# A one-core FNet and low-rank mixer kernel: warm-up products, evacuation, W2's queue and the residual table rearranged in the front

## The chip, the cores and the metric

The kernel runs on one core of one Trainium2 chip. The metric is the device time in microseconds of that core, as the median of several runs. A profiled execution gives the times of single instructions, measured from its own first instruction.

## What is computed

The input x has shape (8, 3136, 256). An FNet layer takes the real part of the two-dimensional Fourier transform over sequence and channels; a mixer follows, with a low-rank product over the sequence (U of 3136 x 32, V of 32 x 3136) and a two-layer MLP over the channels (256 to 1024 to 256), each with its residual:

```
X = np.fft.fft(np.fft.fft(x, axis=1), axis=2).real
h = X.transpose(0, 2, 1) @ U @ V
u = X + h.transpose(0, 2, 1)
out = u + np.maximum(u @ w_ch1, 0) @ w_ch2
```

## The kernel before

The sequence length 3136 is split as 49 x 64 (N1, N2). The transform is done as products with tables of sines. Those tables are made on the chip: VectorE or GpSimd computes an angle as an integer phase, a bit mask takes it modulo a full turn (mask_bits, L427), and ScalarE's sine gives the table (sin_of, L431). The eight batches are handled as four pairs. The first batch of pair 0 goes through a front of its own, because nothing else can cover it; from pair 0's second batch on, the stages are placed between the MLP products of the batches before (plan, L731).

The order of the instructions is written out by hand: manual_schedule (L456) leaves each engine's instructions in the order of the program. So an instruction that waits holds everything that comes after it on its engine or queue. SP and GpSimd issue most loads; GpSimd also computes.

The front (L458 to L675) runs in this order:

- X0, the first batch, is loaded in pieces by load_single (L104), most of them from GpSimd's queue. U is loaded into uf, cast into ub by ScalarE (L525 to L527). Then TensorE gets 28 products of 128 columns into a scratch tile (L533), whose values nobody uses.
- VectorE computes the angles of the tables ua (L536 to L553), Fs and F32 (L557 to L577), ScalarE takes the sines (L555, L569, L578). TensorE multiplies ua with ub (upss) and transposes ua (tpss), 25 products each (L585 to L590). line32 (L198) forms line 32 of the batch with F32; its output lies in a free corner of tpss. Nine unused products follow in tps0 (L594). ScalarE copies upss to us, VectorE copies tpss to T (L595 to L597) and mirrors it (L598).
- quarter_products (L214) are 64 products on X0 for each of four rounds r, into the tiles tps. Each tile is evacuated into one of the staging tiles zts (L609), two rounds to each; then quarter_rows (L236) copies them with a shift of rows into g0, eight copies for each staging tile (L612, L613). Round r's evacuation alternates between VectorE and ScalarE.
- The staging tiles zts and the raw W1 tiles w1_f share memory (the tags w1_f0 and w1_f1), so that each half of W1 (L621) can be loaded only when its staging tile has been read. GpSimd's order here is: a one-element copy that waits for the first evacuation (gate, L615), two loads of V (L616, L617), the two halves of W1. W2 is loaded from SP's queue (L622).
- Six unused products of 512 columns (L646) precede te_single (L293), which multiplies g0 with us; te_out (L267) copies the result into te, and spread (L302) repeats te into the lower half of g0. v_rows (L625) fills T's lower half from V: rows 0 to 8 on ScalarE, the rest on GpSimd.
- lines (L324) are the sequence products of the first eight columns, in four groups: once with g0's upper half (L654), then with te (L657); after each group, move (L334) copies it to q. w1_fold (L636) multiplies W1 with a channel transform table Q, and ScalarE scales it into W1p (L642). w2_fold (L515) adds and subtracts the two halves of W2 on VectorE.
- residual_tables (L442) computes on GpSimd the phases qa of the table Bp and its signs sg; bp_mask and bp_sin are its mask on VectorE and its sine on ScalarE. Then X1, the pair's second batch, is loaded from GpSimd's queue (L669 to L673).

The main loop takes chunks of up to 512 columns of q: mlp1 (L372) makes four pairs of product tiles hps with W1p, each of which ScalarE turns into hT by a ReLU (L382); mlp2 (L384) multiplies hT of the chunk before with W2 and q with Bp, and stores the result. Scratch tiles in PSUM of the front come from a pool of four buffers (bank2, L474), handed out in turn; a tile waits until the readers of the tile four before it are done.

Of the kernel before, what the change touches and what calls it, by code (L numbers as in the profile page):

```python
# [22 lines left out]
def kernel(  # L23
# [9 lines left out]
    nc = tc.nc  # L33
# [3 lines left out]
    P = 128  # L37
# [17 lines left out]
    F32 = cpool.tile([PR, 3, 32], FP16)  # L55
# [16 lines left out]
    def copy_act(o, i):  # L72
        nc.scalar.copy(o, i)  # L73

    def copy_dve(o, i):
        nc.vector.tensor_copy(o, i)  # L76
# [121 lines left out]
    def line32(b, ps=None, start=True):  # L198
        ps = ps if ps is not None else psd.tile([P, 2, D], FP32, tag="ps", name="ps32")
        o, y = ps[0:32, 0], x32[b]  # L200
        for i, (oc, t, yc) in enumerate([(o[:, 0:129], 0, y[:, 0:129]), (o[:, 1:128], 0, y[:, 255:128:-1]),
                                         (o[:, 129:256], 1, y[:, 1:128]), (o[:, 129:256], 2, y[:, 255:128:-1])]):
            nc.tensor.matmul(oc, F32[:, t], yc, start=(start and i == 0), stop=True, skip_group_check=True)

        def out():
            z32 = cpool.tile([32, D], BF16, name=f"z32_{b}")
            nc.scalar.copy(z32[:], o)
            return z32
        return out

    def row32(g, z32):
        nc.sync.dma_start(out=g[63:64, 0:NK1, :], in_=z32[0:NK1])

    def quarter_products(X, ps, i0, n):  # L214

        for i in range(n):
            for m in range(2):
                for q in range(4):
                    d = 32 * q + i0 + i
                    o = ps[32 * q:32 * q + 32, i]  # L220
                    w = X[0:PR, :, (256 - d if d else 128) if m else d]
                    if d:
                        f, oc = Fs[:, 0:3:2 if m else 1, :, 0:NK1] if m else Fs[:, 0:2, :, 0:NK1], o[:, :, :, 0:NK1]
                    else:
                        f, oc = Fs[:, 0, :, 0:NK1], o[:, m, :, 0:NK1]
                    nc.tensor.matmul(oc, w, f, start=(i % 4 == 0 and m == 0), stop=True, skip_group_check=True)
# [9 lines left out]
    def quarter_rows(g, zt, i0, engines):  # L236

        n = zt.shape[4]
        for q in range(4):
            d0 = 32 * q + i0  # L240
            for c in range(2):
                r = 32 - c
                engines[2 * q + c](g[32 * c:32 * c + r].rearrange("p k (s d) -> p k s d", s=2)[:, :, :, d0:d0 + n],
                                   zt[32 * q:32 * q + r, c])
# [179 lines left out]
    def tmp(shape, name, dt=FP32):  # L424
        return pool.tile(shape, dt, name=name, tag=name)

    def mask_bits(a, bits):  # L427

        nc.vector.tensor_scalar(a.bitcast(I32), a.bitcast(I32), (1 << bits) - 1, None, op0=AL.bitwise_and)

    def sin_of(o, a, bits):  # L431

        nc.scalar.activation(o, a.bitcast(I32), AF.Sin, scale=-2.0 * math.pi / (1 << bits) * (1.0 - 2.0 ** -21),
                             bias=pi[0:a.shape[0]])
# [7 lines left out]
    def residual_tables(eng):  # L442
        pq = cpool.tile([P, 4], FP32, name="pq")
        qa = ypool.tile([P, 2, P], FP32, tag="y", name="qa")
        for blk in range(2):
            o = pq[:, blk:blk + 1]
            eng.tensor_scalar(sg[:, blk:blk + 1], pf[:], 64.5 - blk, None, op0=AL.is_ge)
            eng.tensor_scalar(o, sg[:, blk:blk + 1], -64.0, pf[:], op0=AL.mult, op1=AL.add)
            eng.tensor_scalar(o, o, 2.0 / D, blk / D, op0=AL.mult, op1=AL.add)
            eng.tensor_scalar(pq[:, 2 + blk:3 + blk], sg[:, blk:blk + 1], 0.25, 128.25, op0=AL.mult, op1=AL.add)  # L450
            eng.tensor_scalar(qa[:, blk], jf[:, 0:P], o, pq[:, 2 + blk:3 + blk], op0=AL.mult, op1=AL.add)
        eng.tensor_scalar(sg[:], sg[:], -2.0, 1.0, op0=AL.mult, op1=AL.add)
        return lambda: mask_bits(qa[:], 16), lambda: sin_of(Bp[:], qa[:], 16)
# [20 lines left out]
    def bank2(shape, name):  # L474
        return fpool.tile([P, *shape], FP32, tag="f", name=name)
# [4 lines left out]
    idle = W1m[0][:].rearrange("p a j -> p (a j)")[:, 0:640]  # L480
    nc.vector.memset(idle.bitcast(FP32), 0.0)

    wps = bank2([1024], "warm")
# [31 lines left out]
    def w2_fold(i):  # L515
        nc.vector.tensor_tensor(W2[:, :, i * P:(i + 1) * P], w2_f[:, :, 0], w2_f[:, :, 1],
                                op=(AL.subtract if i else AL.add))

    zts = [pool.tile([P, 2048], BF16, name=f"zt{i}", tag=f"w1_f{i}")[:, 0:64 * NK1].rearrange(
        "p (c k s i) -> p c k s i", c=2, k=NK1, s=2) for i in range(2)]  # L520
    g1 = gpool.tile([P, NK1, D], BF16, tag="g1", name="w2_f")
    w2_f = g1[:, 0:16].bitcast(FP32).rearrange("p (t s) d -> p t s d", s=2)

    ub = tmp([P, NK1, 2, R], "ub", BF16)
# [4 lines left out]
    idn = tmp([64, 64], "idn", FP16)  # L529
    ts(idn[:], jf[0:64, 0:64], pf[0:64], None, AL.is_equal)  # L530

    for i in range(28):
        nc.tensor.matmul(wps[:, 0:P], ub[:].rearrange("p k s r -> p (k s r)")[:, 0:P], idle[:, P:2 * P], start=True, stop=True)  # L533

    pk = tmp([P, 4], "pk")
    ts(pk[:, 0:1], pf[:], -1.0, 127.0)  # L536
# [35 lines left out]
    an2 = tmp([PR, 3, 32], "an2")  # L572
# [2 lines left out]
    for i in range(3):  # L575
        ts(an2[:, i], jf[0:PR, 0:32], pv[:, 6:7], pv[:, 7 + i:8 + i])
    mask_bits(an2[:], 16)  # L577
    sin_of(F32[:], an2[:], 16)  # L578
    mask_bits(jq[:], 16)
    Q = tmp([P, 3, P], "Q", FP32R)  # L580

# [2 lines left out]
    tpss = [bank2([16, 64], "ttps") for i in range(2)]  # L584
    for k in range(NK1):  # L585
        nc.tensor.matmul(upss[k // 16][0:64, k % 16], ua[:, k], ub[:, k], start=(k % 8 == 0), stop=True,
                         skip_group_check=True)
    for k in range(NK1):
        nc.tensor.matmul(tpss[k // 16][0:64, k % 16], ua[0:64, k], idn[:], start=(k % 8 == 0), stop=True,
                         skip_group_check=True)  # L590
    z32 = line32(0, tpss[1][:, 12:16].rearrange("p k (a d) -> p a (k d)", a=1), False)
    tps0 = bank2([8, 2, 2, 32], "tps")
    for i in range(9):
        nc.tensor.matmul(tps0[:, 0].rearrange("p s c k -> p (s c k)"), idle[:, 0:P], idle[:, P:2 * P], start=True, stop=True)  # L594
    for i, (k0, k1) in enumerate([(0, 16), (16, NK1)]):  # L595
        copy_act(usv[:, k0:k1], upss[i][0:64, 0:k1 - k0])
        copy_dve(T[0:64, k0:k1, 0:64], tpss[i][0:64, 0:k1 - k0])  # L597
    nc.vector.tensor_copy(T[0:64, :, 64:128], T[0:64, :, 63::-1])  # L598
    z32 = z32()
    sin_of(Q[:, 0:2], jq[:], 16)  # L600
    nc.scalar.mul(Q[:, 2], Q[:, 1], -1.0)

    g0 = gpool.tile([P, NK1, D], BF16, tag="g0", name="g")
    first.g[0] = g0
    row32(g0, z32)
    for r, evac in enumerate([copy_dve, copy_act, copy_dve, copy_act]):
        ps = bank2([8, 2, 2, 32], "tps") if r else tps0
        quarter_products(X0, ps, 8 * r, 8)
        evac(zts[r // 2][:, :, :, :, 8 * (r % 2):8 * (r % 2) + 8].rearrange("p c k s i -> p s c k i"),  # L609
             ps[:, :, :, :, 0:NK1].rearrange("p i s c k -> p s c k i"))  # L610
        if r == 2:
            quarter_rows(g0, zts[0], 0, [copy_dve] * 8)  # L612
    quarter_rows(g0, zts[1], 16, [copy_dve] * 6 + [copy_act] * 2)  # L613
    gate = tmp([1, 2], "gate")
    nc.gpsimd.tensor_copy(gate[:, 0:1], zts[0][0:1, 0, 0, 0, 0:1])  # L615
    nc.gpsimd.dma_start(out=uv[64:96], in_=moe_V)  # L616
    nc.gpsimd.dma_start(out=uv[96:128], in_=moe_V)  # L617
# [1 line left out]
    for c in range(2):  # L619
        w1_f.append(pool.tile([P, 2, 512], FP32R, name=f"w1_f{c}", tag=f"w1_f{c}"))  # L620
        nc.gpsimd.dma_start(out=w1_f[c][:], in_=moe_w_ch1.rearrange("(h p) j -> p h j", p=P)[:, :, c * 512:(c + 1) * 512])  # L621
    nc.sync.dma_start(out=w2_f, in_=moe_w_ch2.rearrange("(t p) (s d) -> p t s d", p=P, s=2))  # L622
    Vk = uv.rearrange("p (k2 k1) -> p k1 k2", k1=N1)

    def v_rows(lo, hi, act=False):  # L625
# [10 lines left out]
    def w1_fold(c, ps=None):  # L636
        ps = ps or bank2([2, 512], "w1ps")
        for blk in range(2):
            for f in range(2):
                nc.tensor.matmul(ps[:, blk], Q[:, 2 if f and blk else blk], w1_f[c][:, f],  # L640
                                 start=(f == 0), stop=(f == 1))
        nc.scalar.mul(W1p[c][:], ps[:], 0.5)  # L642

    teps = bank2([2, D], "teps")
    for i in range(6):
        nc.tensor.matmul(teps[:].rearrange("p a d -> p (a d)"), idle[:, 0:P], idle[:, P:640], start=True, stop=True)  # L646
    te_single(first, 0, lambda g, te: None, teps)
    s3b0 = list(s3_steps(first, 0, copy_alt))
# [1 line left out]
    groups = [(g, blk) for g in range(2) for blk in range(2)]  # L650
    pst = [bank2([2, 2, 256], "ps") for i in range(2)]
    pss = [pst[i // 2][:, i % 2] for i in range(4)]
# [2 lines left out]
    w1_fold(0)  # L655
    for ps, (g, blk) in zip(pss, groups):
        lines(ps, g, blk, P, tes[0])  # L657
        move(ps, g, blk, copy_dve if blk else copy_act)
    w1_fold(1)
    spread([(nc.vector, 8, 16)])(g0, tes[0])  # L660
# [2 lines left out]
    v_rows(17, NK1)  # L663
    w2_fold(0)
    w2_fold(1)
    bp_mask, bp_sin = residual_tables(nc.gpsimd)
    bp_mask()
    bp_sin()
    loads = load_single(1)  # L669
# [100 lines left out]
    for i in range(len(chunks) + 1):  # L770
        cur = chunks[i] if i < len(chunks) else None
        prv = chunks[i - 1] if i else None
        if cur is not None:
            p = cur.p
# [42 lines left out]
```

## Time and profile before

| | us |
|---|---|
| median of 14 runs | 476.11 |
| lowest, highest | 473.68, 478.27 |
| profiled execution, its own time | 476.77 |
| span of its instructions | 475.0 |
| TensorE (products) busy | 436.1 |
| ScalarE busy | 296.3 |
| VectorE busy | 223.9 |
| GpSimd busy | 144.0 |
| mean granted TensorE clock, as a share of full speed | 0.968 |

An instruction line of the timeline gives the start, the length, the engine, the line of the program, the operation, what it writes and reads, how many were merged, and in brackets how long the engine stood idle before it and who released it. PE is TensorE, PEld its weight loads, DVE VectorE, ACT ScalarE, POOL GpSimd, SP the engine that only issues loads and stores; a q behind the name means its queue. The chain of waits follows the work that ended last back to the start. DMA figures are the busy share of the core's 16 DMA engines and the GB/s that they moved.

### The profile page before, as it was taken

To read this page: it belongs to the slowest core of one execution; us is meant where nothing else is said; L and a number is where in the kernel's file an instruction comes from. 1 tells how busy PE (TensorE), PEld (TensorE's weight loads), DVE (VectorE), ACT (ScalarE), POOL (GpSimd) and SP (SyncE) were. 2 spreads that over 40 slices of the span, in tenths; PEclk is the share of its full clock that TensorE was granted. 3 is DMA by queue.
4 is the path that set the end of the run, shared out by engine and by line. 5 is a ranking of instruction groups with operands and counts; after the bars stand their busy time and mean duration, and the time that the engine had idled before them with its cause. 6 is when DMAs were issued, how large, how long until landed. Compare 5 with 4: busy or idle time off the path is not lost.

```text
span 475.0 us, 10551 instructions
## 1 busy us (share of the span) xinstructions
PE 436.1 (92%) x4167; PEld 315.7 (66%) x4229; DVE 223.9 (47%) x537; ACT 296.3 (62%) x422; POOL 144.0 (30%) x156
## 2 busy tenths in 40 slices
PE   3677899699998998999999999999999999999995
PEld 3654566476775776776777776776777777776773
DVE  7624346777633547545344346647254344311212
ACT  5533688566755565777646656677655656666662
POOL 6168434485133026346060035544050000000000
PEclk9855999999999999999999999999999999999998
DMA  8732775459549355777396365586493333333424
GB/s 148 174 99 43 117 201 148 112 168 248 162 121 228 73 144 145 216 209 221 98 167 162 85 177 157 152 249 188 113 179 69 71 68 68 68 66 73 90 51 89
DMA packets 59714, 64.35 MB, mean 135 GB/s; under 512 B 12902, under 2 KB 52624, under 8 KB 59504
## 3 DMA queue, kind: packets, MB, share of 16 engines
q1 hardware_dynamic: 49904, 42.28, 38.4%
q0 software_dynamic: 7280, 14.70, 13.3%
q10 hardware_dynamic: 2480, 6.69, 3.8%
q8 instruction: 33, 0.54, 0.5%
q14 instruction: 17, 0.14, 0.1%
HBM read 34.62 MB, written 32.19 MB: 141 GB/s over the span
## 4 chain that ended last, share of the span: by engine, by line
PE 72%; DVE 8%; DMA 6%; ACT 4%; issue 4%; POOL 3%; SPq 2%; DVEq 0%; POOLq 0%; ACTq 0%
PE hps L380 29%; PE ops L391 29%; PE ps L322 4%; PE ops L394 4%; DMA out_dram<-ob 4%; ACT hT L382 3%; PE ps L184 2%; SPq L406 2%; DVE g L76 1%; DMA g<-zturn 1%; PE teps L284 1%; DVE ob L402 1%; DVE q L76 1%; DVE yb L135 1%; DVE ob L401 1%
## 5 line engine op out<-in xcount | busy, mean ns | idle before, releaser
L382 ACT ACTIVATE hT<-hps 128x1024 bf16<-128x1024 f32 (+1 forms) x208 | 202.3, 975 | 122.1 <-PE hps L380 113.4
L391 PE MATMUL ops<-W,hT 128*128 128x256 bf16 x1568 | 224.9, 273 | 0.7 <-DVE ob L402 0.3
L391 PEld LDWEIGHTS <-hT 128*128 128x128 bf16 x1568 | 145.1, 98 | 35.4 <-DVE ob L402 0.8
L401 DVE TENSOR_TENSOR ob<-ops,om 128x256 f32<-128x256 f32 (+1 forms) x102 | 42.2, 413 | 193.3 <-ACT om L400 188.2
L380 PE MATMUL hps<-q,W1p 128*128 128x512 bf16 (+1 forms) x420 | 105.7, 362 | 5.3 <-DVE q L76 1.4
L380 PE MATMUL hps<-q,W1m 128*128 128x512 bf16 x351 | 95.4, 379 | 2.1 <-ACT hT L382 0.5
L143 POOL TENSOR_TENSOR y<-xa,xb 98x1020 f32<-98x1020 f32 (+1 forms) x24 | 55.3, 2305 | 124.8 <-DMA xa<-in_x_dram 90.2
L76 DVE CAST q<-ps 128x512 bf16<-128x512 f32 (+2 forms) x120 | 64.4, 558 | 37.7 <-PE ps L322 30.0
L380 PEld LDWEIGHTS <-W1p 128*128 128x128 bf16 x448 | 41.2, 99 | 31.8 <-issue 7.1
L380 PEld LDWEIGHTS <-W1m 128*128 128x128 bf16 x384 | 35.3, 98 | 26.5 <-issue 1.4
L394 PEld LDWEIGHTS <-q 128*128 128x128 bf16 x392 | 38.4, 98 | 20.8
L400 ACT COPY om<-ops 128x256 f32<-128x256 f32 (+1 forms) x102 | 37.1, 364 | 8.4 <-PE ops L391 8.1
L402 DVE TENSOR_TENSOR ob<-ops,om 128x256 f32<-128x256 f32 (+1 forms) x102 | 41.1, 403 | 0.0
L322 PE MATMUL ps<-T,g 128*128 128x128 bf16 (+3 forms) x400 | 38.6, 225 | 1.8 <-DMA g<-zturn 1.3
L306 POOL COPY g<-te 64x1024 int32<-64x1024 int32 (+1 forms) x22 | 22.8, 1082 | 51.7 <-DVE te L270 48.3
L394 PE MATMUL ops<-Bp,q 128*128 128x128 f16 x200 | 38.4, 219 | 0.0
L73 ACT CAST z<-ps 128x512 bf16<-128x512 f32 x48 | 28.2, 587 | 16.0 <-PE ps L184 15.7
L394 PE MATMUL ops<-Bm,q 128*128 128x128 f16 x192 | 36.9, 219 | 0.0
L322 PEld LDWEIGHTS <-g 128*128 128x128 bf16 (+1 forms) x400 | 30.7, 102 | 7.3 <-issue 2.9
L99 POOL DMA_INDIRECT xb<-in_x_dram,idx x24 | 25.5, 1064 | 5.4 <-issue 4.5
L134 DVE TENSOR_TENSOR yb<-y 98x508 bf16<-98x508 f32 (+1 forms) x24 | 24.7, 1030 | 0.9 <-POOL y L143 0.8
L184 PE MATMUL ps<-yb,F 98*128 98x258 bf16 (+1 forms) x108 | 18.9, 265 | 5.4 <-DVE q L76 4.3
(137 smaller groups left out, 224.3 us busy)
## 6 DMA issues: line engine op xcount, KB each, us to landing
out_dram<-ob SPq DMA_DIRECT2D x389, 64.0 KB
xa<-in_x_dram SPq DMA_DIRECT2D x24, 392.0 KB
g<-zturn SPq DMA_DIRECT2D x6, 800.0 KB
zturn<-z ACTq DMA_DIRECT2D x9, 512.0 KB
X<-in_x_dram POOLq DMA_DIRECT2D x4, 384.0 KB, 7.5
X<-in_x_dram POOLq DMA_DIRECT2D x2, 744.0 KB, 8.2
zturn<-z ACTq DMA_DIRECT2D x3, 448.0 KB
w_f<-in_moe_w_ch_dram SPq DMA_DIRECT2D x1, 1024.0 KB
```

What stands on the lines that cost most here:

```text
L73: nc.scalar.copy(o, i)
L76: nc.vector.tensor_copy(o, i)
L143: nc.gpsimd.tensor_tensor(ck.y[:, 0:n, 1:256], ck.xa[:, 0:n, 1:256], rb[:, :, 255:0:-1], op=AL.add)
L184: nc.tensor.matmul(o[..., cs], F[:, 2 * t + i].rearrange("p b k c -> p (b k c)"), y[..., cs], start=first, stop=True, skip_group_check=True)
L322: nc.tensor.matmul(o, lt, r, start=st, stop=True, skip_group_check=True)
L380: nc.tensor.matmul(ps[:, i, 0:n], (W1p if ch.sg > 0 else W1m)[jp // 2][:, blk, j], q[:, blk, c0:c0 + n], start=(blk == 0), stop=(blk == 1))
L382: nc.scalar.activation(ch.h[:, 2 * jp:2 * jp + 2, 0:n], ps[:, :, 0:n], AF.Relu)
L391: nc.tensor.matmul(ps, ch.h[:, j, t * P:(t + 1) * P], W2[:, j, :], start=(j == 0 and (t % 2 == 0 or last)), stop=(j == JT - 1), skip_group ...
L394: nc.tensor.matmul(ps[:, j], q[:, j, tk], (Bp if ch.sg > 0 else Bm)[:, j], start=False, stop=False, skip_group_check=True)
L400: nc.scalar.copy(om[:, 0:n], ch.po[:, 0:n, 1])
L401: nc.vector.tensor_tensor(ob[:, 0:n, 0:P], ch.po[:, 0:n, 0], om[:, 0:n], op=AL.add)
L402: nc.vector.tensor_tensor(ob[:, 0:n, P:D], ch.po[:, 0:n, 0], om[:, 0:n], op=AL.subtract)
```

## The change

The unused products before the tables become six of 512 and twenty of 64 columns. Nine unused products in tps0 give way to twelve in a free corner of the tile tpss[1], ahead of line32. The F32 sine and line32 move between the first and second pair of copies. Of the four evacuations, ScalarE takes three instead of two, and VectorE one; the row copies of the first staging tile follow after round 1 instead of round 2; of those of the second, ScalarE takes three instead of two. The residual table's GpSimd part moves ahead of the quarter products, behind a one-element copy that waits for the mask of an2; its mask and sine stay where they were. W2's load moves from SP's queue to GpSimd's, behind W1. The unused products before te_single become fourteen. The lines with te are issued in one loop, and their moves in another.

```diff
-    for i in range(28):
-        nc.tensor.matmul(wps[:, 0:P], ub[:].rearrange("p k s r -> p (k s r)")[:, 0:P], idle[:, P:2 * P], start=True, stop=True)
+    ubw = ub[:].rearrange("p k s r -> p (k s r)")[:, 0:P]
+    for w in [512] * 6 + [64] * 20:
+        nc.tensor.matmul(wps[:, 0:w], ubw, idle[:, P:P + w], start=True, stop=True)
...
-    sin_of(F32[:], an2[:], 16)
     mask_bits(jq[:], 16)
...
-    z32 = line32(0, tpss[1][:, 12:16].rearrange("p k (a d) -> p a (k d)", a=1), False)
+    for i in range(12):
+        nc.tensor.matmul(tpss[1][:, 9:11], idle[:, 0:P], idle[:, P:2 * P], start=True, stop=True, skip_group_check=True)
     tps0 = bank2([8, 2, 2, 32], "tps")
-    for i in range(9):
-        nc.tensor.matmul(tps0[:, 0].rearrange("p s c k -> p (s c k)"), idle[:, 0:P], idle[:, P:2 * P], start=True, stop=True)
     for i, (k0, k1) in enumerate([(0, 16), (16, NK1)]):
         copy_act(usv[:, k0:k1], upss[i][0:64, 0:k1 - k0])
         copy_dve(T[0:64, k0:k1, 0:64], tpss[i][0:64, 0:k1 - k0])
+        if i == 0:
+            sin_of(F32[:], an2[:], 16)
+            z32 = line32(0, tpss[1][:, 12:16].rearrange("p k (a d) -> p a (k d)", a=1), False)
...
+    gate = tmp([1, 2], "gate")
+    nc.gpsimd.tensor_copy(gate[:, 1:2], an2[0:1, 0, 0:1])
+    bp_mask, bp_sin = residual_tables(nc.gpsimd)
...
-    for r, evac in enumerate([copy_dve, copy_act, copy_dve, copy_act]):
+    for r, evac in enumerate([copy_dve, copy_act, copy_act, copy_act]):
...
-        if r == 2:
+        if r == 1:
             quarter_rows(g0, zts[0], 0, [copy_dve] * 8)
-    quarter_rows(g0, zts[1], 16, [copy_dve] * 6 + [copy_act] * 2)
-    gate = tmp([1, 2], "gate")
+    quarter_rows(g0, zts[1], 16, [copy_dve] * 5 + [copy_act] * 3)
...
-    nc.sync.dma_start(out=w2_f, in_=moe_w_ch2.rearrange("(t p) (s d) -> p t s d", p=P, s=2))
+    nc.gpsimd.dma_start(out=w2_f, in_=moe_w_ch2.rearrange("(t p) (s d) -> p t s d", p=P, s=2))
...
-    for i in range(6):
+    for i in range(14):
         nc.tensor.matmul(teps[:].rearrange("p a d -> p (a d)"), idle[:, 0:P], idle[:, P:640], start=True, stop=True)
...
         lines(ps, g, blk, P, tes[0])
+    for ps, (g, blk) in zip(pss, groups):
         move(ps, g, blk, copy_dve if blk else copy_act)
...
-    bp_mask, bp_sin = residual_tables(nc.gpsimd)
```

## The prediction

> **What bounds the kernel now.** I read the overview slices first, then the chain of waits, then the timeline of the front, then the clock by window.
>
> The overview has TensorE busy nine tenths or more in most slices of 11.9 us, but not in the first five and the eighth, and the granted clock at half speed in slices three and four (24 to 48 us):
>
> ```profile
> PE   3677899699998998999999999999999999999995
> ...
> PEclk9855999999999999999999999999999999999998
> ```
>
> So after 50 us the kernel is one long TensorE program, and a microsecond won in the front should reach the end. What ends the front? The chain of waits, in order of time (start, length, what), around the start of the main loop:
>
> ```profile
> 31.97 2.07 POOL T L498
> ...
> 35.26 2.07 POOL T L498
> ...
> 37.40 0.68 POOL sg L447
> ...
> 38.18 2.26 POOL pq L448
> ...
> 43.09 0.42 DVE qa L429
> ...
> 43.95 1.01 ACT hT L382
> ```
>
> GpSimd copies V's rows into T until 37.3, then builds the residual table (37.40 to 43.05), VectorE masks it, ScalarE takes the sine, and only then comes the first ReLU of the main loop. The timeline shows who was ready earlier:
>
> ```profile
> 38.02 2.36 DVE L516 TENSOR_TENSOR W<-w_f 128x1024 bf16<-128x1024 f32 x2
> ...
> 39.39 0.59 PE L380 MATMUL hps<-q,W1p 128*128 128x512 bf16 x1 [1.11 <-ACT W1p L642]
> ...
> 43.53 0.51 ACT L433 ACTIVATE Bp<-qa,pi 128x256 f16<-128x256 int32 x1 [4.20 <-DVE qa L429]
> ...
> 43.95 1.92 ACT L382 ACTIVATE hT<-hps 128x1024 bf16<-128x1024 f32 x2
> ```
>
> The products for that ReLU began at 39.39; ScalarE stood 4.20 us at the sine, which is ahead of the ReLU in its order. **The first ReLU, at 43.95, is the mark against which I cost everything.** The clock, in windows of 1 us (PE, PEld, DVE, ACT, POOL busy, clock, DMA):
>
> ```profile
> 14.00:15.00 1.00, 0.57 (x6) 0.57 (x6) 0.97 (x3) 1.00 (x3) 0.00 (x0) 0.71 0.04 5
> ...
> 17.00:18.00 1.00, 1.00 (x63) 1.00 (x57) 0.86 (x1) 0.00 (x0) 0.00 (x0) 0.58 0.41 122
> ...
> 24.00:25.00 1.00, 0.39 (x2) 0.00 (x0) 0.96 (x4) 0.00 (x0) 0.67 (x1) 0.83 0.42 96
> ...
> 48.00:49.00 1.00, 1.00 (x5) 0.43 (x4) 0.45 (x1) 0.40 (x1) 0.41 (x2) 0.72 1.10 222
> ```
>
> A clock that is 1 or 0.5 must have switched at 14.42 (down), 17.84 (up), 24.66 (down) and 48.56 (up) to give these means. The distances are 1, 2 and 7 times 3.41 us.
>
> [...] the table's first pq step took 2.26 us under the W2 fold, its twin at 41.81 took 0.27; and the W1 load issued at 24.33 moved little until VectorE's row copies ended at 25.99 (39 GB/s at 25 to 26 us, 225 in the next). [...]
>
> **The change, part by part.**
>
> *Early warm-up (L533).* 28 products (3.17 us, 7.16 to 10.33) become 6 of 512 and 20 of 64 columns. From 113 ns for 128 columns there, 6 x 4 x 0.107 + 20 x 0.055 = 3.7 us, to 10.9; the next operand (ua) is ready at 10.87. Cost 0 to 0.3 us, hidden by the sine.
>
> *Order on ScalarE at 12 us.* The us copy no longer stands behind the F32 sine (12.83). Fs ends at 11.93, so us (1.27 us) runs 12.0 to 13.2 instead of 13.2 to 14.39, and the bank of tps0 is free 1.2 us sooner. The nine products of L594 (1.12 us) leave the path; twelve others stand at 12.8 to 14.1 at the latest, in another bank, in front of line32. Quarter products start at about 14.0 instead of 15.48; X0 must have landed, and its traffic falls away at 13 to 14 us. Gain 1.5 us; with the half clock of 14.42 to 17.84 avoided, up to 0.8 more.
>
> *Evacuation and row shifts.* Before: VectorE did two evacuations (0.99 each) and 14 row copies (0.36), the last ending at 25.99. Now r0 is VectorE's, r1 to r3 ScalarE's (0.83). With 64 products in 1.13 to 1.4 us: r1 done at 16.3, evacuated at 17.1; eight row copies to 20.0; r3 evacuated at 19.4; then VectorE 5 x 0.36 to 21.9, ScalarE 3 x 0.86 to 22.0. g0 complete at 22.0 instead of 26.0: gain 4.0 us.
>
> *Fourteen 512-column products (L646).* 14 x 0.22 = 3.0 us at full clock from 18.6: to 21.6, hidden by the row copies. Without that cover: 6.0 us at half clock, and a stall like the 2.28 us that TensorE showed at 21.1 with no releaser. Then they end at 27.
>
> *te, lines, W1 folds.* At full clock te_single is about 1.7 us (50 took 1.59 to 1.7 at 89.92) against 2.89; lines 0.9 (four took 0.22 at 50.75) against 1.78; a fold, at twice the clock, 1.0 against 2.07. Splitting lines from moves removes TensorE's waits of 1.20 and 0.67 us on ScalarE's copies. Summed from 22.0: te 23.7, W1 fold 26 (W1's first half issued at 20.1 when zt0 is free, 4.7 us to land as before), lines 27, second fold 28; ScalarE after V's rows (26.7): first W1p 27.7, two moves to 28.9, second W1p to 29.9. Main products could begin at about 30 instead of 39.4, and a ReLU at 31.
>
> *Residual table early.* Its twelve GpSimd instructions cost 5.65 us where they stood; the uncontended half (41.49 to 43.05) says 3.3 in all. From 13.0, after the gate on an2 (12.79), they end at 16.5 to 17.2, in GpSimd's idle time (9.6 to 18.2). Queued behind them: V's loads, whose own gate opens at about 16.4. They go out at 17.2 instead of 18.33, land 7.1 us later at 24.3, and V's first rows (2.4 us on ScalarE) are done by 26.7. On the late side GpSimd goes from V's rows straight to X1's loads: X1 is issued at about 33 to 36 instead of 43.65; it landed at about 55 (last issue 47.8, 7.5 to land), 9 us ahead of its first use at 64.58, and that moves up with everything.
>
> *W2 behind W1.* The issue leaves SP (0.44 us; nothing stands behind it there until the stores at 54.38) and joins GpSimd's queue after W1's second half, which waits for zt1 (22.0). W1 goes out at 22.0 to 22.8, W2 to 23.6; the spread behind it waits for te (24.5) anyhow: 0 us. But the landing matters: the mask on VectorE stays behind the two W2 folds, and the sine and every ReLU behind the mask. No row shows W2 from this queue. Bounds: 1.05 MB of W1 took 26.0 to 30.7 (223 GB/s); X1's small rows ran at 167 GB/s (1.6 MB, 44.5 to 54.1); at best 300, as at 18 to 21 us. After W1 ends at about 26.8, W2 needs 3.5 to 6.3 us: 30.3 to 33.1. I take 5.2, so 32.0[...]. A fold that finds GpSimd in its last V row could be held up to 2.07 us (L498); by 32 those should be over, so I take 0.
>
> **Sum.** W2 32.0 + folds 2.44 + mask 0.41 + sine 0.51 + steps 0.1 = first ReLU at 35.5 instead of 43.95: **8.5 us** earlier. TensorE has then emptied its short queue as it had before, so the same program follows. For the clock I add 0.4: before, 3.6 us of main loop ran cold; if it is warm about 1.2 us go, with a chance of a third, since TensorE idles from about 32 to 36. Total 8.9. 476.77 (span 475.0 + 1.77 around it) - 8.9 = 467.9; the profiled run stands 0.66 above the median of the runs (476.11), so **467.2**.
>
> **Rivals.** (a) *W2 is not the last to come*: at its best rate it lands at 29.8 to 30.3 and the clock stays up; ReLU at 33.3, 10.7 plus 1.2 of clock: 11.9 us, 464.2. For: DMA ran above 300 GB/s for W2. Against: not from this queue. (b) *Cold front*: the unexplained stall recurs, [...] the fourteen products run at half clock to about 27; te 2.9, lines 1.8, fold 2.07, lines 1.7, fold 2.05, ScalarE 1.0, first products 1.7: ReLU at 40.2, gain 3.7; half a microsecond less if W1 waits too: about 472.8. For: 100% busy from 28.1 to 31.5 did not raise the clock. Against: fourteen dense products are what the slack of 18.6 to 22 has room for. (c) *Slower*: W2 queued last on GpSimd comes so late that it holds the folds, the mask, the sine and all ReLUs. It decides alone from a landing at 40.5; each microsecond later costs one. At 42.5, 2 us lost: 478.1. For: that queue fell to 63 and 32 GB/s at 49 to 51 us. Against: it would need 1.05 MB at under 77 GB/s from 26.8 on. (d) *Nothing left*: the gain is used up by VectorE and ScalarE in 80 to 100 us, where TensorE is 66 to 84% busy; 476. Against: those waits (DVE g, DVE yb) are on instructions in program order, which move with it.
>
> **Chances.** Forecast 0.54, (a) 0.20, (b) 0.16, (c) 0.05, (d) 0.05. Range: W2's bounds give 465.5 to 468.3; (a) comes in whole, and (b) by half, so that with (c) and (d) 0.18 stays out: 463.0 to 472.5. Against the 0.3% (1.4 us) that a measurement can tell: faster 0.90, same 0.05, slower 0.05.
>
> **What would show it.** Right: last g copy near 22, te_single there, residual instructions at 13 to 17, no 1.2 us wait between the te lines, a ScalarE wait at the sine that ends with VectorE's fold and mask, which wait for W2's DMA; first ReLU at 33 to 36. Wrong: teps products at 0.43 us spacing or a gap among them, te_single after 25; a fold ready long before the ReLU (then T's rows or hT's memory hold it); a first ReLU 8 us sooner with an unchanged end.

## The result and the profile after

The changed kernel takes 471.64 us (median of 10 runs, 467.01 to 476.37) against 476.16 (47 runs) for the kernel before, a ratio of 0.9893 with a 95% interval of 0.9863 to 0.9923: 1.1% faster, 4.5 us between the medians. The ratio is of the fast runs alone, those no more than 1.5% above the fastest of their kernel, which leaves out two of the ten, so it is not the quotient of the medians. The gain is half of the 8.9 us forecast; the time lies in the upper half of the range. The profiled execution took 473.46 us, 1.8 more than the median, with a span of 471.7: 3.3 us less than the one of before.

The overview slices of the changed kernel:

```profile
PE   3685898799999999999999999999999999999995
...
PEclk9988999899999999999999999999999999999998
```

The two slices at half clock are gone, but in slice four (35 to 47 us) TensorE is busy to five tenths only. The chain of waits around the first ReLU (start, length, what):

```profile
33.81 2.06 POOL T L498
...
37.45 3.98 POOL T L498
...
41.46 1.03 ACT hT L382
```

The residual table has left the chain (no sg, pq, qa). But the first ReLU comes at 41.46, not at 35.5: only 2.5 us before the 43.95 of the kernel before. What lies behind the ReLU is as long as it was: 475.0 - 43.95 = 431.0 us before, 471.7 - 41.46 = 430.2 after. (In twelve of the fourteen executions profiled here it is 428.9 to 431.3 us; a_dum6 has 432.6 and b_res 434.5.) So the question is the front. There the timeline of TensorE shows this:

```profile
20.81 0.39 PE L651 MATMUL teps<-W1m 128*128 128x512 bf16 x1
...
24.81 4.44 PE L651 MATMUL teps<-W1m 128*128 128x512 bf16 x12 [3.60 <-issue]
...
29.17 1.02 PE L298 MATMUL teps<-g,us 64*32 64x129 bf16 x30
```

Behind the first of the fourteen unused products TensorE stands for 3.60 us, for which the profile names no releaser ("issue"). The other thirteen (the trace has the records of twelve) take 4.44 us, 0.34 each, and te_single starts at 29.17, though g0's last row copy ended at 24.37. The clock in windows of 1 us (the sixth figure after the engines' busy times):

```profile
25.00:26.00 1.00, 1.00 (x4) 0.40 (x3) 0.00 (x0) 1.00 (x2) 1.00 (x2) 0.56 0.44 139
...
28.00:29.00 1.00, 1.00 (x5) 0.30 (x3) 0.00 (x0) 0.00 (x0) 0.00 (x0) 0.73 0.82 182
...
42.00:43.00 1.00, 0.47 (x2) 0.19 (x2) 0.00 (x0) 1.00 (x2) 1.00 (x2) 0.59 0.00 0
...
45.00:46.00 1.00, 1.00 (x7) 0.47 (x5) 0.69 (x1) 0.94 (x2) 1.00 (x2) 0.70 1.17 238
```

By the same reckoning as in the prediction it fell at 25.12, rose at 28.54, fell at 42.18 and rose at 45.60: steps of 3.42, 13.64 and 3.42 us, so again 1, 4 and 1 times 3.41. TensorE was busy for 0.31 of the 3.41 us up to the first fall and for none of the 3.41 us up to the second. From 25.12 to 28.54 the unused products kept it busy throughout, at a granted clock of 0.50, and then the clock rose. a_shift, the kernel below without a gap at this place, was granted 1.00 from 14 to 38 us. A busy stretch alone does not account for the rise: from 28.10 to 31.50 in the kernel before TensorE was busy for all of 3.40 us, and the clock stayed at 0.50. The end of the front in the timeline:

```profile
36.45 3.14 DVE L516 TENSOR_TENSOR W<-w_f 128x1024 bf16<-128x1024 f32 x2
...
37.45 3.97 POOL L498 TENSOR_SCALAR T<-uv,vs 64x512 bf16<-64x512 f32 x1
...
39.51 1.17 DVE L429 TENSOR_SCALAR qa<-qa 128x256 int32<-128x256 int32 x1
...
40.72 0.51 ACT L433 ACTIVATE Bp<-qa,pi 128x256 f16<-128x256 int32 x1 [4.92 <-DVE qa L429]
```

The W2 folds take 3.14 instead of 2.36 us, GpSimd's last V row 3.97 instead of 2.06, the mask 1.17 instead of 0.41: rows and folds lie on each other, which they did not before, since V's rows were then done at 37.3 and the folds began at 38.0.

### The profile page after: what moved, and what is told of

Same layout as the page of the kernel before. It is cut to its first block, busy times and chain, and to the rows that moved or that the text cites. A ratio compares the mean times of both kernels' runs of the same rounds, so it can differ in the third digit from the quotient of the medians.

```text
span 471.7 us, 10568 instructions
## 1 busy us (share of the span) xinstructions
PE 433.8 (92%) x4176; PEld 311.5 (66%) x4238; DVE 223.3 (47%) x535; ACT 298.2 (63%) x424; POOL 142.4 (30%) x158
## 4 chain that ended last, share of the span: by engine, by line
PE 67%; DMA 8%; DVE 7%; ACT 5%; SPq 4%; issue 4%; POOL 3%; DVEq 0%; POOLq 0%; ACTq 0%
PE hps L380 28%; PE ops L391 27%; DMA out_dram<-ob 5%; SPq L406 4%; PE ops L394 3%; PE ps L322 3%; ACT hT L382 2%; PE ps L184 2%; DMA X<-in_x_dram 2%; DMA xa<-in_x_dram 2%; ACT g L73 2%; DVE ob L402 2%; DVE ob L401 1%; PE teps L284 1%; DVE yb L134 1%
## 5 line engine op out<-in xcount | busy, mean ns | idle before, releaser
L380 PE MATMUL hps<-q,W1p 128*128 128x512 bf16 (+1 forms) x420 | 104.0, 358 | 8.4 <-ACT hT L382 4.4
L394 PEld LDWEIGHTS <-q 128*128 128x128 bf16 x392 | 38.5, 98 | 20.9 <-issue 0.3
```

What stands on the lines that cost most here:

```text
L380: nc.tensor.matmul(ps[:, i, 0:n], (W1p if ch.sg > 0 else W1m)[jp // 2][:, blk, j], q[:, blk, c0:c0 + n], start=(blk == 0), stop=(blk == 1))
L394: nc.tensor.matmul(ps[:, j], q[:, j, tk], (Bp if ch.sg > 0 else Bm)[:, j], start=False, stop=False, skip_group_check=True)
```

## The experiments

Of each kernel's profiled execution I read two marks: the start of te_single and the first ReLU. Each ratio is to the kernel before on the same chip. The median of the kernel before differed between the groups (477.36, 478.53 and 477.88 us), so ratios are compared, not times.

| kernel | te_single | first ReLU | between | median us | ratio, 95% interval |
|---|---|---|---|---|---|
| before | 26.05 | 43.95 | 17.90 | 476.16 | 1 |
| changed | 29.17 | 41.46 | 12.29 | 471.64 | 0.9893 (0.9863 to 0.9923) |
| no unused products (a_dum0) | 24.35 | 39.14 | 14.79 | 469.0 | 0.9856 (0.9774 to 0.9938) |
| six of them (a_dum6) | 27.57 | 40.37 | 12.80 | 470.34 | 0.9849 (0.9784 to 0.9913) |
| ten early products (a_shift) | 23.79 | 36.92 | 13.13 | 468.74 | 0.9812 (0.9732 to 0.9892) |
| W2 on SP again (a_w2sp) | 30.47 | 42.75 | 12.28 | 476.0 | 0.9979 (0.9955 to 1.0003) |
| V's last rows on ScalarE (a_vact) | 30.73 | 41.02 | 10.29 | 471.93 | 0.9871 (0.9793 to 0.9949) |
| sine of Bp early (a_mask) | 30.77 | 43.06 | 12.29 | 474.31 | 0.9920 (0.9898 to 0.9942) |
| early products, early sine, V on ScalarE (a_combo2) | 24.53 | 35.52 | 10.99 | 465.93 | 0.9742 (0.9665 to 0.9819) |
| table late again (a_reslate) | 26.89 | 43.34 | 16.45 | 478.15 | 0.9991 (0.9962 to 1.0021) |
| before, table early (b_res) | 27.50 | 42.87 | 15.37 | 476.29 | 0.9957 (0.9933 to 0.9982) |
| before, W2 behind W1 (b_w2) | 26.72 | 44.62 | 17.90 | 475.59 | 0.9945 (0.9916 to 0.9974) |
| early products, early sine, V on VectorE (a_vdve) | 24.78 | 33.47 | 8.69 | 464.68 | 0.9709 (0.9665 to 0.9754) |
| changed once more (a_again) | 29.65 | 41.94 | 12.29 | 474.13 | 0.9897 (0.9863 to 0.9932) |

The first mark moves by 1.6 us between executions in which the front up to there is the same (changed, a_again, a_vact, a_mask); the column "between" hardly does (12.28 to 12.29 in changed, a_again, a_mask and a_w2sp). So the front has two parts, and each experiment speaks to one of them. The change lost 3.1 us in the first part (te_single at 29.17 instead of 26.05) and won 5.6 in the second. Each mark is of one execution; that of a_dum6 was the slowest of its four runs.

**Theory.** The first part is late because TensorE runs out of instructions behind the first unused product, the clock falls, and the remaining products then stand in front of te_single. In the changed kernel the second part is set by GpSimd's last V row, stretched by the W2 folds. **Rivals:** the unused products pay for themselves; W2's landing or the sine behind the folds sets the ReLU, as the prediction had it.

**The gap: ten early products (a_shift).**

```diff
-    for w in [512] * 6 + [64] * 20:
+    for w in [512] * 8 + [64] * 2:
```

> The changed kernel with ten early warm-up products (8 of 512 columns, 2 of 64) instead of 26: about the same time on TensorE, but 16 weight loads and 16 products fewer, 32 instructions. Theory A, in the form that the gap is TensorE's instruction supply, which comes in blocks (the two gaps, at 17.5 and 21.2 us, lie 127 products with their weight loads apart, about 256 instructions): the gap moves 32 instructions on, from behind the first of the fourteen unused products to inside te_single, the fourteen run at 20.8 to 24 at full clock, te_single starts at 24.4 to 25 and te_out ends at 27 to 27.5; first ReLU at 37 to 38.5 and 3 to 5 us less time than the changed kernel. Theory B, that the gap is bound to the place (the second product into teps waits for something there) or to the time: it stays between the first and the second unused product, te_single at 29, same time as the changed kernel.

TensorE's timeline in that kernel:

```profile
18.33 1.92 PE L226 MATMUL tps<-Fs,X 98*32 98x100 f16 x111 [1.25 <-issue]
...
20.18 3.19 PE L651 MATMUL teps<-W1m 128*128 128x512 bf16 x14
...
23.79 0.27 PE L298 MATMUL teps<-g,us 64*32 64x129 bf16 x3 [0.41 <-ACT g L73]
...
24.69 1.51 PE L298 MATMUL teps<-g,us 64*32 64x127 bf16 x47 [0.64 <-issue]
```

The fourteen products run without a break in 3.19 us, 0.23 each, at full clock (1.00 from 20 to 24 us), under the row copies: what the prediction had said of them. The gap has gone into te_single, behind its third product, and is 0.64 us long there, because te_single had to wait for g0 anyhow. Between the two gaps lie 111 + 14 + 3 = 128 products, with 128 weight loads 256 instructions; in the changed kernel 127 + 1 = 128 too. So the gap begins at a count of instructions, not at a place. The profile has a DMA queue that fits:

```profile
q8 instruction: 33, 0.54, 0.5%
```

33 packets with 0.54 MB in all are 16 KB each. The page of the changed kernel counts 4238 weight loads and has the records of 4176 products; with a product to each load that is 8476 instructions, 257 for each packet. The DMA view by tenths of a microsecond gives the time of each packet, and the gaps end with them: in all fourteen executions both gaps end 2.1 to 3.1 us behind a packet of this queue, however early or late it comes. For the second gap the packet and the end are 19.9 and 22.55 in a_reslate, 20.6 and 23.36 in the kernel before, 21.7 and 24.81 in the changed one, 22.0 and 24.69 in a_shift, 23.0 and 25.81 in a_w2sp. So a gap that merely belongs to a time (24.8 here and 24.7 there) is unlikely, and TensorE waiting for its next instructions is my reading, which fits all of them. The profile names no releaser, and what makes a packet late is not seen.

te_single starts 5.4 us earlier than in the changed kernel; the first ReLU, expected at 37 to 38.5, comes at 36.92. It comes there behind the sine (36.51) as the prediction had it, since the folds began only when W2 landed, at 32.95, and GpSimd's row was done at 34.94; so the second part is 0.8 us longer. The ratio is 0.8% lower, 3.9 us, within the 3 to 5 expected, but the intervals overlap: by its time alone a_shift is not clear of the changed kernel, a_vdve, which contains it, is.

**The fourteen products (a_dum0, a_dum6).**

```diff
-    for i in range(14):
+    for i in range(0):
```

This is a_dum0; a_dum6 has range(6).

> The changed kernel without any unused product ahead of te_single (14 to 0). Theory A: in the changed kernel TensorE stood without instructions from 21.2 to 24.8 us, the clock then fell to half, and the other twelve unused products (4.4 us) kept te_single back to 29.2, though g0 was complete at 24.4. Without them te_single starts at 24.5 to 25.0, all of it at half clock (te 2.9, lines 1.8, fold 2.1): te_out ends near 28.5 instead of 31.5, GpSimd's rows of V start 3 us sooner, and the first ReLU is at 38.5 to 40 instead of 41.5; time 1.5 to 3 us less than the changed kernel, some of it lost again since the clock stays low until the main loop is dense. Theory B: the unused products pay for themselves, since they bring the clock up at 28.4; without them everything to the first ReLU runs at half clock and the ReLU comes at 41.5 or later, time the same or up to 2 us more.

> The changed kernel with 6 unused products ahead of te_single, as in the kernel before (14 to 6). Theory A: five products after the gap at half clock take 2.1 us, te_single starts at 26.9 (26.05 in the kernel before), at half clock, te_out ends near 30.5, so about 1 us less than the changed kernel at the first ReLU (40.5) and 0.5 to 1 us in time. Theory B: no gain or a loss of 1 us, because the clock is then not back up at 28.4 and te, lines and folds cost 3 us more than with fourteen.

Without them te_single starts at 24.35, behind g0 (and a gap of 0.59 us behind its first product, again at the 128th), but all to the first W1 fold is at half speed (49 products of te_single take 2.85 us, where 47 took 1.51 in a_shift; the fold takes 2.07 instead of 1.20): 14.79 us to the ReLU instead of 12.29. The ReLU is 2.3 us earlier in that execution, as theory A had it, and with six 1.1 us. In time neither can be told from the changed kernel (0.9856 and 0.9849 against 0.9893, intervals overlapping). So at this place fourteen products with a gap under them bring no more than none: by the marks they cost 4.8 us ahead of te_single and win 2.5 behind it.

**W2's queue (a_w2sp, and alone on the kernel before, b_w2).**

```diff
-    nc.gpsimd.dma_start(out=w2_f, in_=moe_w_ch2.rearrange("(t p) (s d) -> p t s d", p=P, s=2))
+    nc.sync.dma_start(out=w2_f, in_=moe_w_ch2.rearrange("(t p) (s d) -> p t s d", p=P, s=2))
```

b_w2 is the opposite edit of the same line in the kernel before.

> The changed kernel with W2 loaded from SP's queue again, so that it goes out at about 16.5 us beside V. The prediction held W2's landing for the last to come. In the changed kernel's profile its traffic ends at 32 us but VectorE reaches the fold only at 36.4. Theory A (te and then GpSimd's rows are last): W2 by itself costs nothing, V may land 1 to 2 us later than 24.7, first ReLU within 0.7 us of 41.5, time within 1 us of the changed kernel. Theory B (the prediction's: W2's landing is on the path): W2 early brings the first ReLU forward by 2 us or more.

> The kernel before with another part alone: W2 loaded behind W1 from GpSimd's queue. Theory A (W2 from SP costs where it lengthens TensorE's gap in front of te_single; in the kernel before that gap, 21.1 to 23.4, lies under the row copies to 26.0): no more than 1 us of gain, and 0 to 1.5 us of loss if W2 lands later than the folds' start at 38. Theory B (W2 from SP costs by itself, by holding up V and W1, as 4 us between the changed kernel and the one with W2 back on SP suggest): V's first rows at 24.5 instead of 26.6 and 2 to 4 us less time.

Theory A was wrong in both: W2 back on SP gives up 0.9% of the 1.1%, and its move alone is worth 0.55%, about 2.6 us, theory B's 2 to 4. Theory B of a_w2sp was wrong as well, since the ReLU is not earlier. In the second part of the front nothing changes, 12.28 and 17.90 us as without the edit, so the landing of W2 is not on the path in either. What differs in the traces lies in the first part:

```profile
25.81 4.73 PE L651 MATMUL teps<-W1m 128*128 128x512 bf16 x13 [5.32 <-issue]
...
28.15 1.21 ACT L633 CAST T<-uv 64x576 bf16<-64x576 f32 x1 [4.50 <-DMA uv<-in_moe_V_dram]
```

With W2's megabyte issued at 17.08 us the gap is 5.32 us, and V's first rows start at 28.15 instead of 24.69; in b_w2 they start at 24.10 instead of 26.63, as theory B had it. But the marks do not show the time: te_single at 30.47 in a_w2sp is within the 29.17 to 30.77 of changed, a_again, a_vact and a_mask, and at 26.72 in b_w2 it is later than before. That the 2.6 and 4 us are won in the first part is therefore argued, not shown. In the executions with W2 on SP the gap was 2.28 (before), 5.03 (b_res) and 5.32; with W2 behind W1 it was 2.58 to 4.60 in seven. That the load delays the instructions' own DMA fits two of the three, but not the 2.28, and no run took the load away altogether: how the gap's length comes about stays open.

**The second part (a_vact, a_mask).**

```diff
-    v_rows(17, NK1)
+    v_rows(17, NK1, True)
```

```diff
     v_rows(0, 9, True)
+    bp_mask()
+    bp_sin()
...
     w2_fold(1)
-    bp_mask()
-    bp_sin()
```

The first is a_vact, the second a_mask.

> The changed kernel with V's last rows (17 to 24) copied by ScalarE, which stood idle from 35.8 to 40.7 us, instead of by GpSimd (1.4 and 4.0 us there, under the W2 folds). Theory A: the first ReLU waits for GpSimd's last row, which reads front memory that hT is given, and the folds and the mask (3.1 and 1.2 us instead of 2.4 and 0.3) are stretched by that row as well. Then ScalarE's two copies end at 38, the folds at 38.8, the mask at 39.2, and the first ReLU comes at 39.6 to 40.2 instead of 41.5, set by the sine of Bp: 1.3 to 1.8 us less. Theory B: only the sine of Bp behind W2's folds sets it and those are not stretched by GpSimd: first ReLU still at 41 to 41.5.

> The changed kernel with the mask and the sine of Bp moved ahead, behind V's first rows on ScalarE (about 27 us), so that they no longer stand behind the W2 folds. Theory A (the first ReLU waits for GpSimd's last V row as well): with the sine gone, ScalarE still waits for that row at 41 us, first ReLU at 40 to 41.5 and the time within 1 us of the changed kernel. Theory B (the prediction's: folds, mask and sine set the first ReLU): it comes when its products are done, at 37 to 37.5, and the time is 4 us less.

The sine early changes nothing: 12.29 us, and ScalarE waits 5.66 us for GpSimd's row, with the sine long done:

```profile
26.59 0.51 ACT L433 ACTIVATE Bp<-qa,pi 128x256 f16<-128x256 int32 x1
...
39.05 3.97 POOL L498 TENSOR_SCALAR T<-uv,vs 64x512 bf16<-64x512 f32 x1
...
43.06 1.94 ACT L382 ACTIVATE hT<-hps 128x1024 bf16<-128x1024 f32 x2 [5.66 <-POOL T L498]
```

With that row on ScalarE the folds are back at 2.36, the mask at 0.28, and the ReLU comes 10.29 us behind te_single, 2.0 less, and now behind the sine (from 40.60). So theory A holds: in the changed kernel GpSimd's last row comes last, the sine just ahead of it. Its clock time in that execution, 41.02, is outside the 39.6 to 40.2 expected, because te_single began 1.6 us later than in the changed kernel. Neither edit moves the time clearly by itself (0.9871, 0.9920).

**The table (a_reslate, and alone, b_res).**

```diff
-    bp_mask, bp_sin = residual_tables(nc.gpsimd)
...
     w2_fold(1)
+    bp_mask, bp_sin = residual_tables(nc.gpsimd)
```

b_res moves the same line, with its gate, early in the kernel before.

> The changed kernel with the residual table's GpSimd part where it was before, behind the W2 folds and V's last rows. Theory A (GpSimd is on the path from te to the first ReLU in the changed kernel): its 3.3 us without collision, or 5.6 with the folds, come back in full behind 41.4 us: first ReLU at 44.5 to 46, time 3 to 4.5 us above the changed kernel, 475 to 476. V's loads go out no earlier, since they wait for the first evacuation (17.6), not for the table. Theory B: something else sets the first ReLU, and the table late costs under 1 us.

> The kernel before with one part of the change alone: the residual table's GpSimd part early, behind the wait on an2's mask. Theory A (GpSimd's table was the last thing ahead of the first ReLU there, and behind it come the folds): the sine of Bp then follows the W2 folds and the mask (40.4 + 0.4 + 0.5), first ReLU at 41.3 to 42.5 instead of 43.95, and up to 43 if the folds run under GpSimd's rows; time 1 to 2.6 us below the kernel before. Theory B (the table was covered): same time within 0.7 us.

Put back late, the table comes behind GpSimd's last row (39.14), takes until 42.4, and the ReLU follows 16.45 us behind te_single, 4.2 more than in the changed kernel. The ratio loses 1.0%, 4.7 us, a little over the 3 to 4.5 expected; the ReLU itself, at 43.34, is under the 44.5 expected, since the gap was short in that execution (2.58 us). Alone in the kernel before, the early table takes 2.5 us off the second part (17.90 to 15.37) and 0.43%, 2.0 us, off the time: within the 1 to 2.6 expected. Its ReLU is at 42.87, over the 41.3 to 42.5 expected, since te_single began 1.45 us later there.

**All together (a_combo2, a_vdve).** a_combo2 has the ten early products, V's last rows on ScalarE and the early sine. a_vdve has VectorE copy them instead, straight behind te:

```diff
     te_single(first, 0, lambda g, te: None, teps)
+    nc.vector.tensor_copy(T[64:128, 17:NK1, 0:64], Vk[64:128, 17:NK1, :])
+    ts(T[64:128, 17:NK1, 64:128], Vk[64:128, N1 - 17:N1 - NK1:-1, :], vs[64:128], None)
```

> The changed kernel with all three: ten early warm-up products, V's last rows on ScalarE, mask and sine of Bp ahead. Theory A (three things in a row held the first ReLU: the instruction gap with the half-clock products, the GpSimd row, the sine behind W2's folds): te_single at 24, main products at 31.5, ScalarE's V rows to 33.5, first ReLU at 33 to 34.5; time 7 to 9 us below the changed kernel, near 464. Theory B (the main loop's beginning is bound by something else, such as X1's landing or W2's, near 33 to 36 us): the ReLU is early but the time falls by no more than with the shift alone, near 468.

> As the version with the ten early products and the early sine, but V's last rows are copied by VectorE right behind te, while it waits for the first lines, instead of by ScalarE behind the second W1p (there ScalarE's copies of 2.2 us ended at 35.4 and the first ReLU came at 35.5, its products being done at about 34.3). Theory A (ScalarE's rows were the last of the chain): first ReLU when its products are done, 1 to 1.5 us sooner, and 0.5 to 1.5 us less time. Theory B: VectorE's copies collide with GpSimd's and hold up the moves of the lines; no gain.

a_combo2's ReLU is at 35.52, 1 us later than expected: a first fold at half clock (2.07 us), and ScalarE busy with V's rows to 35.4. Its ratio is 1.5% below the changed kernel's, 7.2 us, within the 7 to 9 expected. In a_vdve it is at 33.47:

```profile
31.04 2.27 POOL L498 TENSOR_SCALAR T<-uv,vs 64x512 bf16<-64x512 f32 x1
...
33.47 1.02 ACT L382 ACTIVATE hT<-hps 128x1024 bf16<-128x1024 f32 x1 [1.24 <-POOL T L498]
```

Again the ReLU comes right behind GpSimd's last V row, now the middle ones, and not when its products are done, as theory A had it. The time is 464.68 us, a ratio of 0.9709 (0.9665 to 0.9754): 9.5 us below the changed kernel on the same chip, 13.2 below the kernel before. The difference between a_combo2 and a_vdve (0.3%) is within their intervals. With a_vdve a_combo2's theory B (X1 or W2 bind the main loop's start, so that the time is that of the shift alone) falls. Its own theory B, that VectorE's copies collide with GpSimd's and gain nothing, falls for the ReLU, which is 2.0 us sooner, and is open for the time. This version beats both kernels.

**The changed kernel once more (a_again).**

> The changed kernel once more, beside the others on this chip, as the one to compare them with. Both theories: 0.989 of the kernel before; the gap behind the first of the fourteen products again, of 2 to 4 us.

0.9897 (0.9863 to 0.9932), and a gap of 4.60 us, a little over the 2 to 4 expected.

## Why the prediction was right in direction and half in size

*The frame held.* The front's gain goes to the end in full: 431.0 us from the first ReLU to the end before, 430.2 after. Rival (d), that the gain is used up in 80 to 100 us, falls, and so does the slower one, (c), since W2 landed long before 40.5. What failed lies ahead of the ReLU, which came 6.0 us later than forecast: 2.4 for g0, 4.8 between g0 and te_single, and 1.2 less behind it (12.3 us instead of 13.5).

*The table early* was rightly placed in GpSimd's idle time: its eleven instructions ran from 13.0 to 16.6 (predicted end 16.5 to 17.2), and the two experiments give 2.0 and 4.7 us for it. *The lines* ran as predicted as well, all sixteen with te in one stretch of 1.02 us from 32.67, without the waits of 1.20 and 0.67. Their share was not run apart, nor that of the early products' new widths and of the third evacuation on ScalarE.

*Quarter products.* Predicted at about 14.0, started at 15.36: TensorE waited 1.02 us for X0's DMA. The condition was written down, and then not taken into the sum. A second gap of 1.13 us, at 17.54, lies 128 products before the other. So g0 was complete at 24.37 instead of 22.0: 2.4 us of the loss.

*The step that failed most* is "14 x 0.22 = 3.0 us at full clock from 18.6: to 21.6, hidden by the row copies". They ran from 20.81 to 29.2, through a gap of 3.60 us and then, for 3.4 us, at half clock, and te_single started 4.8 us behind g0. The kernel before showed the gap (2.28 us at 21.1, no releaser); I named it and left it to rival (b), where it belonged in the forecast: removing and adding instructions by the dozen does not remove a wait that came 128 products with their weight loads, 256 instructions, behind the one before. Shifting it by 32 instructions made the step true as it was predicted. Rival (b), 472.8 us, was the nearest; its te, lines and folds at half clock were wrong, because the clock was back at 28.54, behind 3.42 us of dense products. The three took 5.5 us instead of the 10.5 that it charged, and the wait for GpSimd's row, which it did not have, made up most of the difference: that its number came so near, and that the time fell within the range for which half of (b) was let in, is in part luck.

*W2 as the last.* It landed at 33.4 (8.0 us after its issue at 25.37) instead of 32.0, but VectorE came to the folds only at 36.45. In a_shift, with te on time, the folds did wait for W2 (1.09 us, until 32.95). So the term was right for a front that was not there. And the end of the sum was wrong in kind: the ReLU waits for GpSimd's last V row as well. The prediction had this among the signs of being wrong. It set the collision of that row with the folds at 0, since the rows were to be over by 32; with te late they ran to 41.4, and the collision cost 1.9 us of the row, 0.8 of the folds and 0.8 of the mask.

*W2's queue* was given 0 us apart from the landing, an assumption of mine that no trace had shown. The two edits give 2.6 and 4 us. They change the queue and the time of the load together (issued at 17.08 in a_w2sp, at 25.37 in the changed kernel), so which of the two counts is not shown.

*The clock term* of 0.4 us was small beside this: before, the clock was low from 24.66 to 48.56 without a break, after it for two stretches of 3.42 us.

## What to carry to other kernels

A wait of TensorE that nothing in the profile releases, and that comes back after the same count of instructions (here 128 products with their weight loads), can be foreseen: before costing what stands behind it, count to the next one, and place it under a wait that is there anyway. Unused products that are to keep the clock up must run in the time that they are to fill (a_shift: 3.19 us under the row copies, te_single at 23.79); behind a gap they become the thing waited for (changed: 3.60 us of gap, 4.44 of products, te_single at 29.17). And take the front apart at a mark that all kernels share (here te_single and the first ReLU), since the two parts vary on their own: here one by 1.6 us between executions, the other by hundredths.

## What the runs showed of the hardware that was not expected

- In the front TensorE stood still twice with no releaser in the profile, 128 products with their weight loads apart, most of them short (17 to 22 ns each): gaps of 0.2 to 1.6 us the first time and 2.3 to 5.3 us the second. Where fourteen products at full clock or the wait for g0 filled part of the second (a_shift, a_combo2, a_vdve, a_dum0), 0.4 to 0.6 us of it were left. The second gap ended between 24.7 and 25.8 us in all but two executions (22.55 in a_reslate, 23.36 in the kernel before), whatever stood in it. In all fourteen both gaps ended 2.1 to 3.1 us behind a packet of the instruction queue; what sets the packet's time is open.
- VectorE's W2 folds and GpSimd's V rows took longer where they overlapped, mostly the one that began second. Single instructions of the changed kernel show it:

```profile
35.94 1.43 POOL L636 CAST T<-uv 64x512 bf16<-64x512 f32 x1
...
36.45 2.00 DVE L516 TENSOR_TENSOR W<-w_f 128x1024 bf16<-128x1024 f32 x1
...
38.38 1.21 DVE L516 TENSOR_TENSOR W<-w_f 128x1024 bf16<-128x1024 f32 x1
```

The first fold, begun under GpSimd's copy, took 2.00 us instead of 1.22; GpSimd's row, begun at 37.45 under that fold, took 1.9 us longer than its 2.06, nearly the time for which the folds still ran; the second fold, begun under that row, took 1.21. In a_shift the row began first and lost nothing:

```profile
32.89 2.05 POOL L498 TENSOR_SCALAR T<-uv,vs 64x512 bf16<-64x512 f32 x1
32.95 2.18 DVE L516 TENSOR_TENSOR W<-w_f 128x1024 bf16<-128x1024 f32 x1 [1.09 <-DMA w_f<-in_moe_w_ch_dram]
```

Two instructions do not go by the order alone: the copy at 35.94 took 1.43 us instead of 1.09 although it began ahead of the fold (VectorE's copy of te ran beside it, from 35.73 to 36.42), and the mask, begun at 39.51 under the row, took 1.17 instead of the 0.28 of a_vact but ended before the row did (40.68 against 41.42). Why one of the two engines holds up the other the traces do not show.
